# Output weights of seven heads laid out with 32 rows in a partition, and attention output brought into that layout by selecting matmuls

## The chip, the core and the metric

The kernel runs on one core of one Trainium2 chip, in one launch. The metric is the time of an execution on the device, in microseconds. The core has a matmul engine (PE, with its weight loads shown as PEld), a vector engine (DVE), a scalar engine (ACT), GpSimd (POOL), a sync engine that issues DMAs (SP), and 16 DMA engines that serve its queues.

## The reference

One token is decoded. A grouped-query attention over a long cache and a gated feed-forward layer are mixed by one scalar gate. All tensors are bfloat16.

```python
# x (1,1,448); k_cache, v_cache (1,8,65536,256); wq (448,4096); wo (4096,448)
q = (x @ wq).reshape(1, 1, 16, 256).transpose(0, 2, 1, 3)     # 16 query heads
k = jnp.repeat(k_cache, 2, axis=1); v = jnp.repeat(v_cache, 2, axis=1)
p = softmax(einsum("bhqd,bhkd->bhqk", q, k) / 16)
o = einsum("bhqk,bhkd->bhqd", p, v)
a = o.transpose(0, 2, 1, 3).reshape(1, 1, 4096) @ wo
gate = x @ W_gate; up = x @ W_up                              # (448,1792) each
b = (gate * (gate > 0) * up) @ W_down                         # (1792,448)
g = sigmoid((x * gate_w).sum(-1))
out = g * a + (1 - g) * b
```

The two caches hold 537 MB of the 549 MB that are read; `wo` is 3.67 MB.

## The kernel before

The caches are walked head by head (eight cached heads, two query heads each). A head has four K tiles and four V tiles of 16,384 cache rows; a tile is 128 partitions with 64 KB each. Three ring buffers of one tile's size hold them: V tiles use buffer 0 and K tiles alternate between buffers 1 and 2; at the end the last four V tiles use 1 and 2 and `wo` uses buffer 0.

A K tile is transposed on DVE in place, in eight parts (L470), and multiplied by the query on PE (L481, into the PSUM banks `ST`). DVE takes the maximum (L624) and ACT the exponential with the row sums (L626). After a head's fourth K tile comes the head change: the maxima of the partitions are combined (L631 to L640), the probabilities rescaled (L646) and transposed on PE (L651), and the head's sums are combined, by a product with ones (L671) and a reciprocal into `rc` (L672, L674, two columns, one for each query head, with the gate's factor multiplied in). The V tiles are multiplied by the probabilities on PE (L519) into the bank `OP`, in four groups of four partitions.

The output of a head is finished one head later, inside the next head change. DVE copies `OP` to `o_sb` as bfloat16 (L540). Four small products with the selecting columns `emat` (L545, `f_otr`) sum the four partition groups and turn the output so that it stands along partitions, into `T_ps`. DVE multiplies by `rc` and writes four columns of `attnT` (L550, `f_norm`): two columns for each of the two query heads, because partition p holds the output elements 2p and 2p+1. `wo` is loaded in the same way, 256 rows of it to a block with two rows in each of 128 partitions, which is runs of 2 x 896 B:

```python
WO = [(0, 2 * NW), (2 * NW, J - 4), (J - 4, J - 2), (J - 2, J - 1), (J - 1, J)]   # blocks, J = 16, NW = 5
wo_sb[:, lo:hi, :, :], A_wo[lo * 256:hi * 256, :].rearrange("(j p s) n -> p j s n", p=128, s=2)
```

Every product with `wo` (L492, `proj`) multiplies one column of `attnT` by a 224-column half of a `wo` row, accumulating into `A_ps`, two halves in two column groups; the feed-forward result has been put into the same bank early (`f_dn`).

The order of the work is a plan: each operation has an engine, a key (a due time in microseconds from a written-out list `order` with the length of each transfer), and the operations it depends on. Each engine runs its operations in the order of the keys and waits on semaphores. SP issues the transfers in the order of the list: the last full V tiles, the first `wo` transfer (ten blocks), the last V tile in five pieces of 64, 32, 16, 8 and 8 rows of a partition (L688), then four more `wo` transfers (2, 2, 1, 1 blocks). PE multiplies the first `wo` blocks before it meets the pieces of V, and the rest behind the last piece, around the turning of the last head's output. The steps of the heads in the middle stand in loops whose addresses come from a register (`roll`).

Of the kernel before, what the change touches and what calls it, by code (L numbers as in the profile page):

```python
# [25 lines left out]
class _Plan:  # L26
# [8 lines left out]
    def op(self, eng, key, fn, deps=(), tag=None):  # L35
        o = _Op(eng, key, fn, deps, tag=tag)
        self.ops.append(o)
        return o

    def dma(self, eng, key, sem, fn, deps=()):  # L40
        if sem not in self.dsem:
            self.dsem[sem] = self.es.enter_context(self.nc.semaphore("d_" + sem))
        o = _Op(eng, key, fn, deps, dma=sem)
        self.ops.append(o)
        return o
# [167 lines left out]
def bass_gated_mix__gqa_block_cached__glu_gated_reglu__decode_kernel(  # L213
# [35 lines left out]
    with es:  # L249
# [26 lines left out]
        RS = sb("rs", [128, NTH], F32)  # L276
        X = sb("hs", [128, 20], F32)
        rc = sb("rc", [128, 2], F32)
        attnT = sb("attnT", [128, H * 4], BF)
        hT = sb("hT", [128, FT], BF)  # L280


# [27 lines left out]
        VT_ps = M_ps[0:2, 0:128]  # L310
        NMR_ps = M_ps[:, 128:129]
        T_ps = M_ps[:, 480:484]
        GB_ps = M_ps[:, 496:498]
        LS_ps = M_ps[:, 500:502]
        XT_ps = M_ps[:, 504:504 + NX]
# [5 lines left out]
        def mop(*a, **k):  # L321
            o = op(*a, **k)
            touch_m.append(o)
            return o
# [4 lines left out]
        for n in range(3, NT):  # L329
            order.append(("k", n, TILE))  # L330
            if n >= NTH:
                order.append(("v", n - NTH, TILE))
        NW = H - 3
        for i in range(NT - NTH, NT - 1):
            order.append(("v", i, TILE))
        order.append(("wo", 0, 7.3))
        PIECES = [(0, 64), (64, 96), (96, 112), (112, 120), (120, 128)]
        for i, (lo, hi) in enumerate(PIECES):
            order.append(("vp", i, TILE * (hi - lo) / U))

        WO = [(0, 2 * NW), (2 * NW, J - 4), (J - 4, J - 2), (J - 2, J - 1), (J - 1, J)]
        for i in range(1, 5):
            order.append(("wo", i, 0.55 * (WO[i][1] - WO[i][0])))
        t = 3.0
        tL, issue = {}, []
        for kind, i, d in order:
# [15 lines left out]
        for kind, i, _ in order:  # L362
            if kind in ("k", "v") or (kind, i) in (("wo", 0), ("vp", 0)):
                r = place(kind, i)
                slot[kind, i], freed[kind, i] = r, held.get(r, [])
                held[r] = [(kind, i)]
        wo_sb = ring[slot["wo", 0]][:, 0:J * 2 * D].rearrange("p (j s n) -> p j s n", j=J, s=2)


        d_x = dma("ac", -9, "x", lambda e: e.dma_start(x_row, A_x[0, :, :]))  # L370
# [24 lines left out]
            prev = op("gp", 0.3 + 0.01 * w, lambda e, w=w: e.iota(iot1[32 * w:32 * w + 32, :], [[-1, 4]], base=0, channel_multiplier=1), [prev])  # L395
        g_em = op("gp", 0.4, lambda e: e.tensor_scalar(emat[:], iot1[:], 0.0, None, ALU.is_equal), [prev])

        prev = g_em
        for i in range(4):
            prev = op("gp", 0.5 + 0.01 * i, lambda e, i=i: e.tensor_scalar(selc[:, 6 + i:7 + i], iot1[:, 0:1], 4.0 * (i + 1), None, ALU.is_lt), [prev])  # L400
        g1 = op("gp", 0.6, lambda e: e.tensor_tensor(selc[:, 6:7], selc[:, 6:7], selc[:, 8:9], ALU.add), [prev])
# [12 lines left out]
        z6 = mop("pe", 1.6, lambda e: e.matmul(GB_ps, ones_f[0:1, :], gz[0:1, 2:4], start=True, stop=True), [z5, c_one])  # L414
        z7 = mop("dv", 1.7, lambda e: e.tensor_copy(gb[:], GB_ps), [z6])


        def f_xeo(e):
            e.tensor_copy(xeo[0:1, 0:128:2], x_row[0:1, NR3:D])
# [90 lines left out]
        def make_pv(n, lo, hi, sl, tv, dep):  # L510
            h, a = divmod(n, NTH)

            def f_pv(lo, hi):
                return lambda e: f_mm(e, lo, hi)

            def f_mm(e, lo, hi):
                for k in range(lo // 2, hi // 2):
                    g = k % 4
                    ins = e.matmul(OP[32 * g:32 * g + 4, :], pcur[a % 2][:, 4 * k:4 * k + 4],  # L519
                                   ring[sl][:, k * 512:(k + 1) * 512],  # L520
                                   start=False, stop=False, skip_group_check=True,
                                   tile_position=(0, 32 * g))
                return ins
            tp = max(tv, last["tev", h])
            if lo == 0:
                pc[n] = op("ac", tp - 5, lambda e: e.copy(  # L526
                    pcur[a % 2][:].rearrange("p (k i) -> p k i", i=4),
                    ptp[:].rearrange("p (k i f) -> p k i f", i=4, f=4)[:, :, :, a]), last["ev", h] + [pv.get(n - 2)])
            if lo == 0 and a == 0:
                zero_o(last["tev", h] + (0.5 if h else -2), h)  # L530
            deps = [dep, pc[n]] + ([last["zo", h]] if a == 0 and lo == 0 else [])
            if n >= NT - NTH and a == 1:
                for q_, (l2, h2) in enumerate(PIECES):
                    pv[n] = op("pe", tp + 0.1 * q_, f_pv(l2, h2), deps if q_ == 0 else [dep], tag=("tail", 1, q_))
            else:
                tag = ("pv", a % 2, sl) if n < NT - NTH else ("tail", a % 2, 0 if n < NT - 1 else [q_[0] for q_ in PIECES].index(lo))
                pv[n] = op("pe", tp, f_pv(lo, hi), deps, tag=tag)
            if a == NTH - 1 and hi == U:
                tn = tp + (8.0 if n < NT - 1 else 1.2)
                o1 = op("dv", tn, lambda e: e.tensor_copy(o_sb[:], OP[:]), [pv[n], last.get(("otr", h - 1))])  # L540

                def f_otr(e):
                    for s in range(2):
                        for par in range(2):
                            ins = e.matmul(T_ps[:, 2 * s:2 * s + 2], o_sb[:, par * 256 + s:par * 256 + 256:2],  # L545
                                           emat[:, 2 * par:2 * par + 2], start=(par == 0), stop=(par == 1))
                    return ins
                o2 = mop("pe", tn + 0.5, f_otr, [o1, g_em], tag="otr")
                def f_norm(e, at):
                    return e.tensor_tensor(at.rearrange("p (s q) -> p s q", q=2), T_ps.rearrange("p (s q) -> p s q", q=2),  # L550
                                           rc[:, :].unsqueeze(1).to_broadcast([128, 2, 2]), ALU.mult)
                o3 = mop("dv", tn + 1, lambda e: f_norm(e, attnT[:, h * 4:(h + 1) * 4]), [o2, last["rc", h]])
                o3.roll = lambda e, r: f_norm(e, attnT[:, bass.ds(r * 4 - 4, 4)])
                last["ocp", h], last["otr", h], last["norm", h] = o1, o2, o3
                if h < H - 1:
                    last["l4", h + 1].deps.append(o3)
                last["tn", h] = tn + 1

        for kind, i, t in sorted(issue, key=lambda q: q[0] != "wq"):
# [11 lines left out]
            elif kind == "gu":  # L571
# [27 lines left out]
                def f_dn(e):  # L599
                    for ft in range(FT):  # L600
                        ins = proj(e, hT[:, ft:ft + 1], wd_sb[:, ft, :], ft == 0, False)
                    return ins
                l_["dn"] = op("pe", tg + 3, f_dn, [l_["hT"], l_["wd"]])
            elif kind == "wd":
                l_["wd"] = dma("sp", t, "wd", lambda e: e.dma_start(wd_sb, B_W_down.rearrange("(p ft) d -> p ft d", ft=FT)))
            elif kind == "k":
# [22 lines left out]
                if t_ == NTH - 1:  # L629
# [40 lines left out]
                    l2 = op("dv", T + 18.2, lambda e: e.tensor_scalar(X[:, 6:8], selc[:, 0:2], X[:, 5:6], None, ALU.mult), [l1])  # L670
                    l3 = mop("pe", T + 19, lambda e: e.matmul(LS_ps, ones_f[:, :], X[:, 6:8], start=True, stop=True), [l2, c_one], tag="l3")  # L671
                    l4 = mop("dv", T + 19.5, lambda e: e.reciprocal(rc[:, :], LS_ps), [l3])  # L672
                    last["l4", h] = l4
                    l5 = op("dv", T + 19.6, lambda e: e.tensor_scalar(rc[:, :], rc[:, :], gb[:, 0:1], None, ALU.mult), [l4, z7])  # L674
                    last["rc", h] = l5
                    last["tev", h] = T + 20
                    for args in [p_ for p_ in pending if p_[0] // NTH == h]:
# [2 lines left out]
            elif kind in ("v", "vp"):  # L680
                if kind == "v":
                    n, lo, hi = i, 0, U
                    sl = slot["v", n]
                    dep = dma("sp", t, "r%d" % sl, lambda e, sl=sl, n=n: e.dma_start(ring[sl][:], v_src(n)), free(("v", n)))
                else:
                    n, (lo, hi) = NT - 1, PIECES[i]
                    sl = slot["vp", 0]
                    dep = dma("sp", t, ("wq", "wqh", "wd", "wf0", "wf1")[i], lambda e, sl=sl, n=n, lo=lo, hi=hi: e.dma_start(  # L688
                        ring[sl][:, lo * 256:hi * 256], v_src(n)[:, lo * 256:hi * 256]), free(("vp", 0)))
                args = (n, lo, hi, sl, tL[kind, i], dep)  # L690
                if ("tev", n // NTH) in last:
                    make_pv(*args)
                else:
                    pending.append(args)
            elif kind == "wo":
                lo, hi = WO[i]
                l_["wo", i] = dma("sp", t, "wo%d" % i, lambda e, lo=lo, hi=hi: e.dma_start(
                    wo_sb[:, lo:hi, :, :], A_wo[lo * 256:hi * 256, :].rearrange("(j p s) n -> p j s n", p=128, s=2)), free(("wo", 0)))

        LAST = last["tn", H - 1]  # L700
        for i, (lo, hi) in enumerate(WO):
            for h in range(lo // 2, (hi + 1) // 2):
                key = max(tL["wo", i], last["tn", h] + 0.5) + 0.01 * h
                if i == 0:
                    key = tL["vp", 0] - 1 + 0.01 * h
                if i in (1, 2):
                    key = LAST - (0.7, 0.2)[i - 1]
                elif i > 2:
                    key = LAST + 2 + 0.1 * i

                def f_wo(e, h=h, lo=max(lo, 2 * h), hi=min(hi, 2 * h + 2)):
                    for j in range(lo, hi):
                        for s in range(2):
                            c = h * 4 + s * 2 + j - 2 * h
                            ins = proj(e, attnT[:, c:c + 1], wo_sb[:, j, s, :], False, j == J - 1 and s == 1)
                    return ins
                fin = op("pe", key, f_wo, [l_["wo", i], last["norm", h], l_["dn"]])
        f0 = op("dv", T_END, lambda e: e.tensor_copy(fin_o[:, 0:D2], A_ps[0:1, 0:D2]), [fin])
        f1 = op("ac", T_END, lambda e: e.copy(fin_o[:, D2:D], A_ps[32:33, 0:D2]), [fin])
        f2 = dma("sp", T_END + 1, "out", lambda e: e.dma_start(out[0, :, :], fin_o), [f0, f1])  # L720
# [30 lines left out]

        @block.vector
        def _(e):
            pl.emit_heads("dv", progs["dv"], e, [first["dv", h] for h in range(2, H)] + [last["ocp", H - 1]], 2)

        @block.scalar
        def _(e):
# [35 lines left out]
```

## Time and profile before

| | |
|---|---|
| median of 3 runs | 1277.62 us (1277.54 to 1278.2) |
| the profiled execution | 1277.72 us |
| its span, first to last instruction | 1275.9 us |
| mean granted TensorE clock | 0.63 |
| PE, PEld, DVE, ACT busy | 32%, 12%, 50%, 6% of the span |
| DMA | 549.17 MB, mean 430 GB/s, the SP queue 99.7% of 16 engines' span |

A page of the profile gives busy times, the span in 40 slices, the queues, and the chain of work that ended last. Further views give windows (busy time of each engine, granted clock, share of the DMA engines and GB/s in a stretch), the timeline (start, length, engine, line, operation, operands, and in brackets the idle time before it and what ended it), groups of instructions by line (busy time in total and mean ns of one, then the idle time before them), and the DMA issues (count, KB, median us from issue to landing). Times in the timeline and windows count from the start of the span.

### The profile page before, as it was taken

Reading aid. Unit: us, or ns where it says so; the run is one execution under the profiler, and the core shown is the slowest. Engines: PE = TensorE matmul, PEld = TensorE weight load, DVE = VectorE, ACT = ScalarE, POOL = GpSimd, SP = SyncE. Lnnn points to the kernel's source line nnn. Section 1 sums busy time; section 2 is a strip of 40 time slices with the busy share of each in tenths; the row PEclk is TensorE's granted clock in tenths of the full one; section 3 lists DMA queues with packets and bytes.
Section 4 is the critical chain, followed back from the end, with each engine's and each line's share of the span. In section 5 each row is a group of like instructions: output and inputs, shape, how many; then the busy total and the mean of one; then the engine's idle time right before and its main releaser. Section 6 shows DMA issues by size and latency. Waiting matters only on the chain.

```text
span 1275.9 us, 10241 instructions
## 1 busy us (share of the span) xinstructions
PE 403.0 (32%) x4500; PEld 147.3 (12%) x4500; DVE 634.6 (50%) x424; ACT 71.9 (6%) x156; POOL 4.1 (0%) x21
## 2 busy tenths in 40 slices
PE   0343433142332223332223431324321243322515
PEld 0211211010110101111001110101100011100202
DVE  4688555553455633556433755335554355554200
ACT  0000100010000100000000100001000010000100
POOL 1000000000000000000000000000000000000000
PEclk9857665566665566656666655666656666556666
DMA  9999999999999999999999999999999999999998
GB/s 400 453 428 429 430 430 438 436 434 431 431 431 440 434 427 436 429 440 438 427 431 434 436 438 431 431 434 431 440 434 427 436 429 438 438 429 431 434 415 359
DMA packets 12944, 549.17 MB, mean 430 GB/s; under 512 B 1283, under 2 KB 3590, under 8 KB 3974
## 3 DMA queue, kind: packets, MB, share of 16 engines
q1 hardware_dynamic: 12930, 549.03, 99.7%
q8 instruction: 6, 0.10, 0.0%
q14 instruction: 4, 0.03, 0.0%
q10 hardware_dynamic: 4, 0.00, 0.0%
HBM read 549.03 MB, written 0.00 MB: 430 GB/s over the span
## 4 chain that ended last, share of the span: by engine, by line
DVE 37%; another core or an unknown queue 28%; DMA 15%; PE 12%; issue 5%; SPq 1%; ACT 0%; DVEq 0%
DVE ring L470 35%; PE ST L481 8%; DMA ring<-in_A_k_cache_dram 8%; DMA ring<-in_A_v_cache_dram 3%; PE O L519 3%; DMA ring<-in_A_wq_dram 2%; DMA ring<-in_A_wo_dram 2%; SPq L688 1%; DVE P_sb L646 1%; DVE nmb L624 1%; PE M_ps L442 1%; DVE o_sb L540 0%; PE M_ps L671 0%; PE A_ps L492 0%
## 5 line engine op out<-in xcount | busy, mean ns | idle before, releaser
L470 DVE STREAM_TRANSPOSE ring<-ring 128x2048 uint32<-128x2048 uint32 x256 | 565.7, 2275 | 408.5 <-DMA ring<-in_A_k_cache_dram 408.5
L481 PE MATMUL ST<-ring,xcur 128*16 128x512 bf16 x2048 | 223.4, 610 | 760.9 <-DVE ring L470 757.9
L481 PEld LDWEIGHTS ST<-ring,xcur 128*16 128x16 bf16 x2048 | 62.6, 119 | 909.3 <-DVE ring L470 800.1
L519 PE MATMUL O<-ring,pcur 128*4 128x512 bf16 x2048 | 141.6, 436 | 45.9 <-DMA ring<-in_A_v_cache_dram 45.9
L626 ACT ACTIVATE P_sb<-ST,nmb 128x512 bf16<-128x512 f32 x32 | 45.3, 1415 | 1040.6 <-DVE nmb L624 1040.6
L624 DVE TENSOR_REDUCE nmb<-ST 128x1 f32<-128x512 f32 x32 | 22.0, 689 | 106.4 <-PE ST L481 106.4
L519 PEld LDWEIGHTS O<-ring,pcur 128*4 128x4 bf16 x2048 | 54.3, 97 | 137.7 <-issue 90.7
L540 DVE CAST o_sb<-O 128x512 bf16<-128x512 f32 x8 | 5.5, 685 | 72.3 <-PE O L519 72.3
L646 DVE TENSOR_TENSOR P_sb<-P_sb,hs 128x1024 bf16<-128x1024 bf16 x16 | 18.9, 1215 | 6.9 <-ACT hs L640 6.9
L651 PE MATMUL PT<-identb,P_sb 128*128 128x128 bf16 x128 | 12.8, 259 | 21.5 <-DVE P_sb L646 21.5
L526 ACT COPY pcur<-ptp 128x256 bf16<-128x256 bf16 x32 | 14.0, 439 | 32.3 <-PE O L519 32.2
L442 PE MATMUL M_ps<-ring,P_sb 128*128 128x256 bf16 x64 | 8.8, 309 | 18.6 <-DMA ring<-in_A_wq_dram 18.6
L637 DVE TENSOR_REDUCE mx<-M_ps 2x1 f32<-2x128 f32 x8 | 2.2, 279 | 22.4 <-PE M_ps L635 22.4
L651 PEld LDWEIGHTS PT<-identb,P_sb 128*128 128x128 bf16 x128 | 9.3, 116 | 23.7 <-DVE P_sb L646 23.7
L660 ACT COPY ptp<-PT 128x256 bf16<-128x256 bf16 x32 | 10.3, 375 | 25.2 <-PE PT L651 25.2
L442 PEld LDWEIGHTS M_ps<-ring,P_sb 128*128 128x128 bf16 x64 | 7.0, 111 | 20.2 <-issue 18.7
L626 ACT ACTIVATION_READ_ACCUMULATOR P_sb<-ST,nmb 128x1 f32 x32 | 8.5, 265 | 0.0
L550 DVE TENSOR_TENSOR attnT<-M_ps,rc 128x4 f32 (+1 forms) x8 | 1.3, 162 | 7.3 <-PE M_ps L671 6.3
L492 PE MATMUL A_ps<-ring,attnT 128*1 128x224 bf16 x64 | 4.7, 305 | 0.6 <-DMA ring<-in_A_wo_dram 0.6
L506 PE MATMUL O<-zer,identb 128*128 128x512 bf16 x8 | 4.7, 593 | 0.0
L671 PE MATMUL M_ps<-hs,ones_f 128*128 128x2 f32 x16 | 4.4, 344 | 0.0
L671 PEld LDWEIGHTS M_ps<-hs,ones_f 128*128 128x128 f32 x16 | 4.2, 315 | 0.1
(81 smaller groups left out, 58.6 us busy)
## 6 DMA issues: line engine op xcount, KB each, us to landing
ring<-in_A_v_cache_dram SPq DMA_DIRECT2D x1, 4096.0 KB, 29.1
ring<-in_A_wq_dram SPq DMA_DIRECT2D x1, 3072.0 KB, 29.0
ring<-in_A_wo_dram SPq DMA_DIRECT2D x1, 2240.0 KB, 39.0
ring<-in_A_v_cache_dram SPq DMA_DIRECT2D x1, 2048.0 KB, 23.0
ring<-in_B_W_down_dram SPq DMA_DIRECT2D x1, 1568.0 KB, 33.1
ring<-in_B_W_gate_dram SPq DMA_DIRECT2D x1, 1344.0 KB, 30.7
ring<-in_B_W_up_dram SPq DMA_DIRECT2D x1, 1344.0 KB, 33.5
ring<-in_A_v_cache_dram SPq DMA_DIRECT2D x1, 1024.0 KB, 25.0
```

The costliest lines, as they stand in the source:

```text
L442: ins = e.matmul(QN_ps, xw3[:, k_, 31 - j:159 - j], rhs, start=(j == 0 and kt == 0), stop=(j == J - 1 and kt == R3))
L470: return lambda e: e.transpose(v, v)
L481: ins = e.matmul(bank[32 * w:32 * w + 16, :], xcur[:, x0:x0 + 16], ktv[sl][:, u0:u0 + 16, c, :, r_], start=(b == 0 and c == 0 and r_ == 0) ...
L519: ins = e.matmul(OP[32 * g:32 * g + 4, :], pcur[a % 2][:, 4 * k:4 * k + 4], ring[sl][:, k * 512:(k + 1) * 512], start=False, stop=False, s ...
L526: pc[n] = op("ac", tp - 5, lambda e: e.copy(pcur[a % 2][:].rearrange("p (k i) -> p k i", i=4), ptp[:].rearrange("p (k i f) -> p k i f", i= ...
L624: smax[n] = op("dv", sx, lambda e, n=n, t_=t_: e.tensor_reduce(NM[:, t_:t_ + 1], ST[n % 2][:], AX.X, ALU.max, negate=True), [qk[n, 1], las ...
L626: aexp[n] = op("ac", sx + 1, lambda e, n=n, t_=t_: e.activation(P_sb[:, t_:2048:4], ST[n % 2][:], ACTF.Exp, bias=NM[:, t_:t_ + 1], scale=1 ...
L646: rsc = op("dv", tt, lambda e, pb=pb: e.tensor_tensor(pb, pb, X[:, 12:16].unsqueeze(1).to_broadcast([128, 256, 4]), ALU.mult), [h7, aexp[n]])
L651: ins = e.transpose(PT[rd][:, s * 128:(s + 1) * 128], P_sb[:, (rd * 8 + s) * 128:(rd * 8 + s + 1) * 128], identb[:, :])
L660: ins = e.copy(dst, src)
L671: l3 = mop("pe", T + 19, lambda e: e.matmul(LS_ps, ones_f[:, :], X[:, 6:8], start=True, stop=True), [l2, c_one], tag="l3")
L688: dep = dma("sp", t, ("wq", "wqh", "wd", "wf0", "wf1")[i], lambda e, sl=sl, n=n, lo=lo, hi=hi: e.dma_start(ring[sl][:, lo * 256:hi * 256], ...
```

## The change

`wo` of heads 0 to 6 is loaded as 112 partitions with 32 consecutive rows each, in two transfers: rows 0 to 23 of every partition ahead of the last V tile, rows 24 to 31 behind its pieces. The runs are 21,504 and 7,168 B. Head 7's two blocks keep the old layout, in two transfers behind that. The attention output has to stand in the new layout: partition 16h + 8q + d, column s, for element 32d + s of query head q of cached head h. For this, `o_sb` is now divided by the row sum while it is copied from `OP` (the factor stands in `rcr`, one value for each partition, made by the mask `mg` and one more reduction), and 16 selecting products with shifted views of the mask `esel` add a head's two outputs into 32 columns of the bank of `A_ps` (`AX_ps`), which one product with zeros clears before the feed-forward result is accumulated there. One copy takes the columns to `attnA` when head 6 is done. Head 7 is turned as before and copied to `attnZ`. In the loops the shifted view of `esel` is addressed from a register.

```diff
+        g_es = op("gp", 0.405, lambda e: e.memset(esel[:], 0.0), [g_em])
+        for par in range(2):
+            g_es = op("gp", 0.41 + 0.01 * par, lambda e, par=par: e.tensor_copy(
+                esel[:, par, 120:129:8], emat[:, 2 * par:2 * par + 2]), [g_es])
...
+        z8 = op("dv", 1.8, lambda e: e.tensor_tensor(mg[:], emat[:, 0:2], emat[:, 2:4], ALU.add), [g_em])
+        z9 = op("dv", 1.9, lambda e: e.tensor_scalar(mg[:], mg[:], gb[:, 0:1], None, ALU.mult), [z7, z8])
...
-                o1 = op("dv", tn, lambda e: e.tensor_copy(o_sb[:], OP[:]), [pv[n], last.get(("otr", h - 1))])
+                o1 = op("dv", tn, lambda e: e.tensor_scalar(o_sb[:], OP[:], rcr[:, 0:1], None, ALU.mult),
+                        [pv[n], last.get(("otr", h - 1)), last["rc", h]])
+                def f_sel(e, w):
+                    for d_ in range(8):
+                        for par in range(2):
+                            ins = e.matmul(AX_ps, esel[:, par, w(d_)], o_sb[:, par * 256 + d_ * 32:par * 256 + (d_ + 1) * 32],
+                                           start=False, stop=False, skip_group_check=True)
...
-                o3 = mop("dv", tn + 1, lambda e: f_norm(e, attnT[:, h * 4:(h + 1) * 4]), [o2, last["rc", h]])
+                if h < HA:
+                    o2 = op("pe", tn + 0.5, lambda e: f_sel(e, lambda d_: slice(120 - 16 * h - d_, 248 - 16 * h - d_)),
+                            [o1, g_es, l_["axz"]], tag="otr")
+                    o2.roll = lambda e, r: f_sel(e, lambda d_: bass.ds(136 - d_ - r * 16, 128))
+                    last["l5", h + 1].deps.append(o1)
+                else:
+                    o2 = mop("pe", tn + 0.5, f_otr, [o1, g_em])
+                    o2 = mop("dv", tn + 1, lambda e: e.tensor_copy(attnZ[:], T_ps), [o2])
...
+                l_["axz"] = op("pe", tg + 2.9, lambda e: e.matmul(
+                    AX_ps, identb[:, :], zer[:, 0:1].to_broadcast([128, 32]), start=True, stop=True, skip_group_check=True),
...
-                    l5 = op("dv", T + 19.6, lambda e: e.tensor_scalar(rc[:, :], rc[:, :], gb[:, 0:1], None, ALU.mult), [l4, z7])
+                    l5 = op("dv", T + 19.6, lambda e: e.tensor_tensor(rc[:, :], rc[:, :], mg[:, :], ALU.mult), [l4, z9])
+                    l5 = op("dv", T + 19.7, lambda e: e.tensor_reduce(rcr[:, :], rc[:, :], AX.X, ALU.add), [l5])
...
-        WO = [(0, 2 * NW), (2 * NW, J - 4), (J - 4, J - 2), (J - 2, J - 1), (J - 1, J)]
+        HA = H - 1
+        PA = HA * 16
+        SA = 24
+        WO = [(0, SA), (SA, 32), (J - 2, J - 1), (J - 1, J)]
...
+                if i < 2:
+                    fn = lambda e, lo=lo, hi=hi: e.dma_start(
+                        wo_a[:, lo:hi, :], A_wo[0:PA * 32, :].rearrange("(p s) n -> p s n", s=32)[:, lo:hi, :])
+                else:
+                    fn = lambda e, lo=lo, hi=hi: e.dma_start(
+                        wo_z[:, lo - J + 2, :, :], A_wo[lo * 256:hi * 256, :].rearrange("(p s) n -> p s n", s=2))
...
+        aA = op("dv", last["tev", H - 1] + 1, lambda e: e.tensor_copy(attnA[:], AX_ps), [last["otr", HA - 1]])
...
+                if i < 2:
+                    for s_ in range(lo, hi):
+                        ins = proj(e, attnA[0:PA, s_:s_ + 1], wo_a[:, s_, :], False, False)
+                else:
+                    for s_ in range(2):
+                        c = s_ * 2 + lo - J + 2
+                        ins = proj(e, attnZ[:, c:c + 1], wo_z[:, lo - J + 2, s_, :], False, i == 3 and s_ == 1)
...
+            fin = op("pe", LAST + 0.5 + i if i else tL["vp", 0] - 1, f_wo, [l_["wo", i], aA if i < 2 else last["otr", HA], l_["dn"]])
```

## What the change was predicted to do

> **What bounds the kernel now.** I read the page first, its span, slices and queues.
>
> ```profile
> span 1275.9 us, 10241 instructions
> POOL 1000000000000000000000000000000000000000
> DMA  9999999999999999999999999999999999999998
> q1 hardware_dynamic: 12930, 549.03, 99.7%
> ```
>
> The 16 DMA engines are busy for 99.7% of the span and nothing is idle in any slice before the last, so the bytes set the time and only what stands after the last bytes is paid besides. The profiled execution took 1277.72 us, 1.82 more than its span; the median is 1277.62. I sum against 1277.72. Then the chain of waits, its end:
>
> ```profile
> 1244.53 26.59 DMA ring<-in_A_wo_dram
> 1271.16 0.91 PE A_ps L492 x8
> 1272.27 1.68 PE A_ps L492 x16
> 1273.97 0.38 DVE P_sb L718
> ```
>
> The end is a wo transfer landing at 1271.16 and then the last wo products. The rate at which the bytes come is read from the table of windows (busy of PE, PEld, DVE, ACT, POOL, then clock, DMA share, GB/s):
>
> ```profile
> 1200.00:1241.00 41.00, 11.54 (x128) 3.73 (x128) 0.00 (x0) 0.83 (x2) 0.00 (x0) 0.62 1.01 434
> 1244.00:1247.00 3.00, 2.48 (x24) 0.83 (x28) 0.00 (x0) 0.00 (x0) 0.00 (x0) 0.50 1.06 381
> 1250.00:1257.00 7.00, 2.82 (x56) 1.96 (x48) 0.00 (x0) 0.00 (x0) 0.00 (x0) 0.99 1.00 431
> 1270.00:1273.00 3.00, 2.38 (x26) 1.03 (x28) 0.85 (x2) 0.00 (x0) 0.00 (x0) 0.50 0.59 216
> ```
>
> V tiles (64 KB in one run per partition) move at 434 GB/s, which is 27.1 for each of 16 engines; the middle of the first wo transfer (runs of 1,792 B) moves at 381 with the engines just as busy. The sizes, and the end in order of time:
>
> ```profile
> ring<-in_A_wo_dram SPq DMA_DIRECT2D x1, 2240.0 KB, 39.0
> ring<-in_A_wo_dram SPq DMA_DIRECT2D x2, 448.0 KB, 26.7
> ring<-in_A_wo_dram SPq DMA_DIRECT2D x2, 224.0 KB, 21.4
> ```
> ```profile
> 1250.74 2.08 PE L492 MATMUL A_ps<-ring,attnT 128*1 128x224 bf16 x40
> 1269.95 0.59 PE L519 MATMUL O<-ring,pcur 128*4 128x512 bf16 x4 [0.69 <-DMA ring<-in_A_v_cache_dram]
> 1270.61 0.69 DVE L540 CAST o_sb<-O 128x512 bf16<-128x512 f32 x1 [72.31 <-PE O L519]
> 1271.16 0.91 PE L492 MATMUL A_ps<-ring,attnT 128*1 128x224 bf16 x8 [0.61 <-DMA ring<-in_A_wo_dram]
> 1272.01 0.27 PE L545 MATMUL M_ps<-emat,o_sb 128*128 128x2 bf16 x4
> 1272.27 1.66 PE L492 MATMUL A_ps<-ring,attnT 128*1 128x224 bf16 x16
> 1272.31 0.16 DVE L550 TENSOR_TENSOR attnT<-M_ps,rc 128x4 bf16<-128x4 f32 x1 [1.01 <-PE M_ps L545]
> 1273.39 0.09 PEld L492 LDWEIGHTS A_ps<-ring,attnT 128*1 128x1 bf16 x4 [0.29 <-DMA ring<-in_A_wo_dram]
> ```
>
> The last piece of V is met at 1269.95, the first wo transfer behind it at 1271.16, the last at 1273.39; 16 products take 1.66 us (104 ns each), and PE ends at 1273.93, which is 3.79 us before 1277.72.
>
> **Part 1: bytes and runs.** All wo bytes stay: 2240 + 2 x 448 + 2 x 224 KB. Ahead of V's pieces stood 2.294 MB, 6.02 us at 381 GB/s; now 112 x 21,504 B = 2.408 MB, at 434 5.55 us, so 0.47 less. Behind the pieces stood 1.376 MB, 3.61 us; now 112 x 7,168 B = 0.803 MB at 434, 1.85 us, and 0.459 MB still in runs of 1,792 B, 1.20 us: 3.05, 0.56 less. Taken alone the transfers end 1.03 us earlier. SP issues fewer packets (2,048 become 112 + 112 + 256), and the long issues below get shorter:
>
> ```profile
> 1230.82 13.67 SPq L688 DMA_DIRECT2D ring<-in_A_v_cache_dram  x5
> 1244.53 16.67 SPq L697 DMA_DIRECT2D ring<-in_A_wo_dram  x4
> ```
>
> They wait for room in the queue while the engines have work (shares of 1.00 and more above) and end at 1261.2, before the transfers are met. I cost that at nothing.
>
> **Part 2: the products at the end.** The transfer met first behind V's pieces was 448 KB, 1.20 us; it is now 1.85. With 0.47 won ahead, it lands at 1271.16 - 0.47 + 0.65 = 1271.34. Only then may its 16 products start, and 8 more for head 7: 24 x 0.104 = 2.49 us, end at 1273.83 against 1273.93. The cast (now a multiplication by one value per partition, 0.69 us either way: same bank, same elements) and the four products of L545 end by 1271.2, the copy of head 7's output is covered by 16 products, and the wo products of heads 0 to 6, 48 instead of 40 with 0.052 us each (2.5 us from 1250.74 on), are over long before the first V piece is met. So 1.03 us of transfers becomes 0.10 us of time: **1277.6**, if the new transfers run at full rate.
>
> **Part 3: what 112 rows do to the 16 engines.** Every transfer of more than one row in this trace has 128 rows, eight to an engine; no row shows 112. I bound it from both sides. The low end is part 2. The other end: the 434 GB/s may be a limit not of the engines but of the partitions that each of them has to itself, which the 128-row rows can't tell apart. The 1.06 beside 381 speaks a little for it: an engine starts a packet while the one before is unfinished, so it isn't the engine's queue alone that holds it. Seven rows in a row to an engine don't line up with groups of eight, so two engines meet in one group and halve each other. If each engine shares all its rows, the big transfer takes 11.10 us (+5.08 against 6.02) and the small one 3.70 (+2.50 against 1.20): it lands at 1278.74, PE ends at 1281.23, 7.30 late: 1285.0. If half of them, 8.33 (+2.31) and 2.78 (+1.58): 1275.05, 1277.54, 3.61 late: 1281.3. I take the middle, **1283.2**. Towards the other neighbours, a shared row of V's first piece (32 KB at 27.1 GB/s) adds 1.2 us; two of them make the upper bound 1287.4.
>
> [...]
>
> **Part 4: the seven head changes.** Each gets 16 selecting products in place of four, the reciprocal of the next row sum waits behind them on PE (L671 follows them), and one more small reduction on DVE follows. First the groups of instructions (busy, mean ns, idle before), then the timeline:
>
> ```profile
> L545 PE MATMUL M_ps<-emat,o_sb 128*128 128x2 bf16 x32 | 2.1, 170 | 1.5 <-DVE o_sb L540 1.1
> L545 PEld LDWEIGHTS M_ps<-emat,o_sb 128*128 128x128 bf16 x32 | 1.5, 107 | 3.6 <-DVE o_sb L540 3.2 <-issue 0.4
> L669 DVE TENSOR_REDUCE hs<-hs 128x1 f32<-128x4 f32 x8 | 1.3, 157 | 0.3
> ```
> ```profile
> 1191.68 0.08 PEld L635 LDWEIGHTS M_ps<-identf,hs 128*2 128x2 f32 x1 [0.44 <-issue]
> 579.53 0.23 DVE L674 TENSOR_SCALAR rc<-rc,gb 128x2 f32<-128x2 f32 x1
> 585.94 4.50 DVE L470 STREAM_TRANSPOSE ring<-ring 128x2048 uint32<-128x2048 uint32 x2 [6.18 <-DMA ring<-in_A_k_cache_dram]
> ```
>
> A product and its load unpipelined are 0.28 us; twelve more are 3.3 us at most, and by the 0.27 us for four above, 0.8 at least. Each also gets a register instruction for its weights' address, which the trace doesn't show alone: 0.44 us at most, by the gap that held one at a loop's end, 7.0 for 16; by the 0.07 us in which a whole product passes, 1.1. Between 2 and 10 us then, with 0.2 for the reduction, and I take 3. Cover at the smallest of these changes that I read is 6.18 us, in which DVE waits for a K tile. If that is gone, DVE starts up to 4 us late on a tile of 17.7 us in a period of 38.7 (two tiles of 8.39 MB at 434 GB/s), and catches up before the next; nothing queued behind it frees a buffer sooner than SP needs it, since a V transfer is issued 33.0 us ahead of landing for 19.3 us of bytes:
>
> ```profile
> ring<-in_A_v_cache_dram SPq DMA_DIRECT2D x31, 33.0
> ```
> ```profile
> 160.01 17.66 DVE L470 STREAM_TRANSPOSE ring<-ring 128x2048 uint32<-128x2048 uint32 x8 [12.39 <-DMA ring<-in_A_k_cache_dram]
> 110.74 3.28 PE L481 MATMUL ST<-ring,xcur 128*16 128x512 bf16 x32 [8.46 <-DVE ring L470]
> ```
>
> Zero, then. The same for head 0, whose extra reduction is followed by 12.39 us of waiting, and for the one product that clears the selected columns, followed by 8.46. The mask and its copies on GpSimd and two small DVE operations fall into the first slice, where GpSimd's only work lies.
>
> **Rivals.**
> A. *The engines are the limit, not the partitions.* Then part 2 stands alone: 1277.6, not slower. For it: V's first piece, in rows of 32 KB, still moves at 431. With the clock at 0.99 instead of 0.50 in the last products (0.052 instead of 0.104 us for 24, -1.25) it would be 1276.4, still not 0.2% away (2.55 us, about what a measurement can tell from no change).
> B. *112 rows go out as 14 engines with eight rows, or the busiest groups take eight rows at the single rate without meeting.* Big transfer 8 x 21,504 / 27.1 = 6.35 us (+0.33), small one 2.12 (+0.92): 1272.41, PE ends at 1274.90, +0.97: 1278.7. It decides where the work splits evenly by groups. [...]
> C. *The head changes lose their cover.* It decides when the selecting products pass some 20 us, the rest of a K period, far over the 10 of part 4. At 1 us each over it, seven make 7 us: 1284.7. Against it stands all of part 4.
>
> **How the numbers follow.** Engines that meet (the forecast, 1281.3 to 1287.4) 0.62: the one mechanism that the transfers' new shape touches directly. No meeting, A: 0.22. B: 0.09. C, or still fewer engines: 0.03. Something I don't see that wins over 2.55 us: 0.04, since all that the transfers' runs can win is 1.03. Slower by over 0.2% is then 0.62 + 0.03 = 0.65; within 0.2%, A and B, 0.31; faster 0.04. The range begins at A less the spread of some 0.4 of single runs, 1277.2, and ends at 1287.4; the likeliest case alone spans 1281.3 to 1287.4.
>
> **What would show it.** In the windows after the last full V tile, the new transfer should show less than 400 GB/s with all engines busy, and packets of 21,504 B well over 0.8 us. V's last piece should be met 2 to 5 us later than 1269.95, measured back from the end, and the idle time before the last wo products should be laid on wo's DMA. Head changes should show DVE still waiting for K's DMA. I am wrong if the new transfer runs near 430 GB/s: then the end moves by 0.1 us, and the products' 2.5 us is the new last step. I am also wrong if the selecting products end after the K tile has landed and the next transfers on SP come late.

## The result, and the profile after

| | before | changed |
|---|---|---|
| median | 1277.74 us (1277.39 to 1278.2, 6 runs) | 1287.24 us (1286.41 to 1288.11, 6 runs) |
| profiled execution | 1277.72 us | 1286.86 us |
| span | 1275.9 us | 1285.1 us |

The changed kernel takes 1.0075 times as long (95% interval 1.0062 to 1.0088), 9.5 us more. I read first whether anything was lost ahead of the `wo` transfers. The windows from the start to 1241 us, before and then after (columns as in the prediction; the last is GB/s):

```profile
0.00:1241.00 1241.00, 385.13 (x4304) 140.79 (x4304) 633.40 (x421) 71.58 (x155) 4.08 (x21) 0.63 1.00 433
```
```profile
0.00:1241.00 1241.00, 401.13 (x4389) 149.47 (x4389) 633.86 (x425) 71.98 (x155) 4.99 (x24) 0.63 1.00 433
```

PE is busy 16 us more, in the head changes, and the bytes come at the same 433 GB/s: no time is lost there. The end of the chain of waits after, and the windows of the last 40 us:

```profile
1233.03 47.61 DMA ring<-in_A_wo_dram
1280.69 2.42 PE A_ps L507 x24
1283.13 0.38 DVE P_sb L745
```
```profile
1246.00:1250.00 4.00, 3.90 (x40) 1.35 (x44) 0.00 (x0) 0.00 (x0) 0.00 (x0) 0.50 0.98 226
1251.00:1255.00 4.00, 0.63 (x12) 0.09 (x4) 0.00 (x0) 0.00 (x0) 0.00 (x0) 1.00 1.05 253
1257.00:1262.00 5.00, 3.66 (x44) 2.50 (x38) 0.00 (x0) 0.00 (x0) 0.00 (x0) 0.68 0.99 426
1274.00:1278.00 4.00, 1.35 (x12) 0.18 (x8) 0.00 (x0) 0.00 (x0) 0.00 (x0) 0.50 1.00 223
```

The chain still ends with a `wo` transfer and the products behind it. But in the first and the last of these windows, where the 112-row transfers run (in the last one together with V's last packets), the DMA engines are as busy as ever (0.98 and 1.00) and move half as much (226 and 223 GB/s). In between, in the third window, V's first piece comes at 426.

The trace also records each DMA packet, with its size, start and length. The 112 packets of 21,504 B took 1.05 to 1.64 us, 1.48 on average, and at least 16 of them were under way at any time in the first window. With the share of 0.98 that shows no engine idle, and every one of these packets is slow, not a few of them: at the 27.1 GB/s of the prediction one would take 0.79 us. The timeline of the end:

```profile
1230.76 2.24 SPq L715 DMA_DIRECT2D ring<-in_A_v_cache_dram  x5
1277.64 0.60 PE L534 MATMUL O<-ring,pcur 128*4 128x512 bf16 x4 [1.74 <-DMA ring<-in_A_v_cache_dram]
1278.29 0.75 DVE L555 TENSOR_SCALAR o_sb<-O,rcr 128x512 bf16<-128x512 f32 x1 [77.10 <-PE O L534]
1279.10 0.27 PE L568 MATMUL M_ps<-emat,o_sb 128*128 128x2 bf16 x4 [0.86 <-DVE o_sb L555]
1280.69 1.66 PE L507 MATMUL A_ps<-ring,attnA 112*1 112x224 bf16 x16 [1.32 <-DMA ring<-in_A_wo_dram]
1282.13 0.96 PE L507 MATMUL A_ps<-ring,attnZ 128*1 128x224 bf16 x8
```

V's last piece is met at 1277.64 instead of 1269.95, 7.69 us later; the transfer behind it 3.05 us after that instead of 1.21, another 1.84 us. From there to PE's end it is 2.40 us instead of 2.77. PE ends at 1283.09 instead of 1273.93: 9.16 us, against 9.14 us between the two profiled executions. So the whole loss lies in the transfers at the end.

### The profile page after: what moved, and what is told of

It is laid out like the page before. It is cut to its first block, busy times and chain, and to the rows that moved or that the text cites. A ratio compares the mean times of both kernels' runs of the same rounds, so it can differ in the third digit from the quotient of the medians.

```text
span 1285.1 us, 10602 instructions
## 1 busy us (share of the span) xinstructions
PE 421.1 (33%) x4593; PEld 157.4 (12%) x4593; DVE 635.2 (49%) x428; ACT 72.3 (6%) x156; POOL 5.0 (0%) x24
## 4 chain that ended last, share of the span: by engine, by line
DVE 37%; another core or an unknown queue 27%; DMA 17%; PE 13%; issue 5%; ACT 0%; SPq 0%; DVEq 0%
DVE ring L485 34%; PE ST L496 8%; DMA ring<-in_A_k_cache_dram 8%; DMA ring<-in_A_wo_dram 4%; DMA ring<-in_A_v_cache_dram 3%; PE O L534 3%; DMA ring<-in_A_wq_dram 2%; PE A_ps L561 1%; DVE P_sb L672 1%; DVE nmb L650 1%; PE M_ps L457 1%; DVE o_sb L555 0%; PE M_ps L697 0%; PE A_ps L507 0%
## 5 line engine op out<-in xcount | busy, mean ns | idle before, releaser
L555 DVE TENSOR_SCALAR o_sb<-O,rcr 128x512 bf16<-128x512 f32 x8 | 6.0, 746 | 77.1 <-PE O L534 77.1
L561 PE MATMUL A_ps<-o_sb,esel 128*128 128x32 bf16 x112 | 18.6, 206 | 4.8 <-DVE o_sb L555 3.7
L561 PEld LDWEIGHTS A_ps<-o_sb,esel 128*128 x112 | 11.8, 105 | 12.7 <-issue 5.5
L507 PE MATMUL A_ps<-ring,attnA 112*1 112x224 bf16 x64 | 5.8, 368 | 6.2 <-DMA ring<-in_A_wo_dram 6.2
L507 PEld LDWEIGHTS A_ps<-ring,attnA 112*1 112x1 bf16 x64 | 3.8, 117 | 8.1 <-DMA ring<-in_A_wo_dram 6.8
```

The lines of the kernel that those rows point to most:

```text
L507: ins = e.matmul(A_ps[32 * g:32 * g + 1, 0:D2], lhsT, rhs[:, g * D2:(g + 1) * D2], start=start, stop=stop, skip_group_check=True, tile_pos ...
L561: ins = e.matmul(AX_ps, esel[:, par, w(d_)], o_sb[:, par * 256 + d_ * 32:par * 256 + (d_ + 1) * 32], start=False, stop=False, skip_group_c ...
```

## Experiments

The theory, which no trace shows directly: the 112 rows fall on partitions that the DMA engines share. The rivals: the shape of the source (long runs that leave gaps), the work added on PE and DVE, and row counts other than 128 as such. They ran in two groups of four, e1 to e4 and e5 to e8, each beside the kernel before on one chip, which took 1277.78 us (1277.45 to 1278.41) in the first group and 1277.97 us (1277.44 to 1278.57) in the second.

**e1_rows128**: 128 rows in the same runs.

```diff
-        wo_a = ring[slot["wo", 0]][0:PA, 0:32 * D]...
+        wo_a = ring[slot["wo", 0]][:, 0:32 * D]...
-                        wo_a[:, lo:hi, :], A_wo[0:PA * 32, :]...
+                        wo_a[:, lo:hi, :], A_wo[0:128 * 32, :]...
...
```

> The two wo transfers bring 128 rows of 32 instead of 112 (the last 16 rows are those of head 7, loaded twice; the products still use 112 partitions). Runs (21,504 and 7,168 B) and their distance in memory (28,672 B) stay. Shared partitions: with eight rows to an engine the transfer runs at about 430 GB/s, 2.75 MB in 6.3 us, and the time falls to about 1278.7 us. Rival, the source: long runs that leave out 7,168 B of every 28,672 are what is slow, so the rate stays near 235 GB/s and the time is 1287 us or, with a seventh more bytes, up to 1289 us.

Measured 1278.73 us, ratio 1.0008 (0.9998 to 1.0018). A window in the first transfer, and the end of the timeline:

```profile
1244.00:1247.00 3.00, 2.79 (x28) 0.96 (x32) 0.00 (x0) 0.00 (x0) 0.00 (x0) 0.50 1.02 437
```
```profile
1270.06 0.60 PE L534 MATMUL O<-ring,pcur 128*4 128x512 bf16 x4 [0.67 <-DMA ring<-in_A_v_cache_dram]
1272.27 1.66 PE L507 MATMUL A_ps<-ring,attnA 112*1 112x224 bf16 x16 [0.48 <-DMA ring<-in_A_wo_dram]
```

One seventh more bytes, and 8.5 us less than the changed kernel. The 128 packets of 21,504 B took 0.80 to 0.81 us each. (Packets are counted in the window in which they start, so a short window can show a little over 434.) The long runs and the gaps in the source are not the cause: that rival falls.

**e2_old_transfers**: all of the change but the transfers.

```diff
-        WO = [(0, SA), (SA, 32), (J - 2, J - 1), (J - 1, J)]
+        WO = [(0, 20), (20, 24), (24, 28), (J - 2, J - 1), (J - 1, J)]
...
-                        wo_a[:, lo:hi, :], A_wo[0:PA * 32, :].rearrange("(p s) n -> p s n", s=32)[:, lo:hi, :])
+                        wo_a.rearrange("p (j s) n -> p j s n", s=2)[:, lo // 2:hi // 2, :, :],
+                        A_wo[lo * 128:hi * 128, :].rearrange("(j p s) n -> p j s n", p=128, s=2))
...
```

> The changed kernel with the transfers of before (128 rows, runs of 1,792 B, 10 + 2 + 2 + 1 + 1 blocks), which leaves the wo rows in other places than the products take them to be; 40, 8, 8, 4 and 4 products. Everything else of the change stays: selecting products, division first, order of the last products. Shared partitions: 1277.9 us (24 products of 0.104 us behind the turning of head 7 instead of 16, +0.2). Rival, the work: if the selecting products and the longer head changes carry part of the loss, the time stays several us higher, up to 1287 us.

Measured 1277.77 us, ratio 1.0 (0.999 to 1.0009). The end of its chain:

```profile
1271.53 2.35 PE A_ps L507 x24
1273.91 0.38 DVE P_sb L746
```

PE ends as in the kernel before, to 0.05 us. The selecting products, the division first and the new order of the last products cost nothing that shows. The rival of the added work falls.

**e3_short_runs**: 112 rows, but the old runs of 1,792 B.

```diff
-                        wo_a[:, lo:hi, :], A_wo[0:PA * 32, :].rearrange("(p s) n -> p s n", s=32)[:, lo:hi, :])
+                        wo_a.rearrange("p (j s) n -> p j s n", s=2)[:, lo // 2:hi // 2, :, :],
+                        A_wo[0:PA * 32, :].rearrange("(j p s) n -> p j s n", p=PA, s=2)[:, lo // 2:hi // 2, :, :])
```

> The changed kernel with 112 rows, but each partition's 32 wo rows come in 16 runs of 1,792 B as in the kernel before, not in one run (which puts them into other places than the products take them to be). Shared partitions: the rate is as low as with the long runs, some 235 GB/s or below, and the time is 1287 us or more. Rival, the source: runs of 1,792 B moved at 381 GB/s before, so 2.408 MB take 6.3 us and 0.803 MB 2.1 us, and the time is about 1278.7 us.

Measured 1286.98 us, ratio 1.0069 (1.0052 to 1.0086), as slow as the changed kernel:

```profile
1245.00:1251.00 6.00, 4.53 (x44) 1.55 (x48) 0.00 (x0) 0.00 (x0) 0.00 (x0) 0.50 1.07 228
```

Runs that moved at 381 GB/s into 128 partitions move at 228 into 112. What is slow is the way into 112 partitions, in runs of 1,792 B as in those of 21,504 B (226).

**e4_rows120**: 120 rows, 15 times 8 (`PA + 8` for `PA` in the two lines of e1's diff).

> The two wo transfers bring 120 rows (8 more than needed); the products still use 112 partitions. 120 is 15 times 8. Shared partitions, in the prediction's words of groups of eight neighbours: each of 15 engines has a group of eight to itself, the rate is 15/16 of 434, 407 GB/s, and the time about 1278.7 us. [...]

Measured 1290.47 us, ratio 1.0101 (1.0084 to 1.0118).

```profile
1245.00:1251.00 6.00, 4.26 (x56) 1.53 (x60) 0.00 (x0) 0.00 (x0) 0.00 (x0) 0.61 0.98 226
```

Fifteen of its packets of 21,504 B are under way between 1246 and 1250 where the changed kernel has 16, as 15 engines with eight rows each would show, and that doesn't help: 226 GB/s. If the eight rows of an engine are neighbours, groups of eight neighbouring partitions, as the prediction had them, are wrong; which rows an engine takes isn't in the trace. What was left to try was the rival that any count but 128 is slow.

**e5_rows64_low and e6_rows64_mid**: each of the two transfers of 112 rows becomes two transfers of 64, which go into partitions 0 to 63 in e5 and into 32 to 95 in e6. If the count alone is the cause, both are as slow as the changed kernel; if the place is, they can differ.

```diff
...
+                    q4 = ring[slot["wo", 0]][0:64, :]          # e6: [32:96, :]
+                    for half, c0 in ((0, 0), (1, 36 * D)):
+                        fn = lambda e, ...: e.dma_start(
+                            q4[:, c0:c0 + 32 * D].rearrange("p (s n) -> p s n", s=32)[:, lo:hi, :],
+                            A_wo[half * 2048:half * 2048 + 2048, :].rearrange("(p s) n -> p s n", s=32)[:, lo:hi, :])
...
```

> The changed kernel, in which each of the two wo transfers of 112 rows is replaced by two transfers of 64 rows, both into partitions 0 to 63 (other columns), 128 rows in all as in e1_rows128; the products take what lies in partitions 0 to 111 of the first, so they are not those of the reference. [...]

> As e5_rows64_low, but the transfers of 64 rows go into partitions 32 to 95, which the products don't all read. Only the place differs. [...] Rival, the row count: as slow as e5_rows64_low, about 1287 us. [...]

Measured: 1292.54 us (ratio 1.0113, 1.0098 to 1.0129) in partitions 0 to 63, and 1278.84 us (1.001, 1.0 to 1.0019) in 32 to 95. A window of the low one, then of the middle one:

```profile
1245.00:1251.00 6.00, 3.21 (x32) 1.10 (x36) 0.00 (x0) 0.00 (x0) 0.00 (x0) 0.50 1.01 208
```
```profile
1244.00:1247.00 3.00, 2.45 (x24) 0.83 (x28) 0.00 (x0) 0.00 (x0) 0.00 (x0) 0.50 1.02 437
```

Same rows, same bytes, same runs, same count: 208 GB/s in one place and 437 in the other, 13.7 us apart. For 64 rows the count as such is not the cause; the place is. And groups of eight neighbours are out, whichever rows an engine takes: partitions 32 to 95 are eight such groups, which at the 27.1 GB/s that 434 leaves to each of 16 would give 217 GB/s, not 437. That 112 and 120 rows are slow for the same reason is inferred from this; no other place was tried for them. An estimate from the two rates: the 3.67 MB of the four transfers take 17.6 us at 208 GB/s and 8.4 at 437, which is 9.2 of the 13.7 us. In the other 4.5, V's packets around the transfers were slowed too (those of 32 KB took up to 2.98 us, in e6 at most 1.23), as in the changed kernel. How much of that each transfer causes I didn't take apart.

**e7_four_rows**: the kernel before, with longer runs but 128 rows.

```diff
...
+                    wo_4[:, lo // 2:hi // 2, :, :], A_wo[lo * 256:hi * 256, :].rearrange("(h p s) n -> p h s n", p=128, s=4)
...
+                    for s in range(4):
+                        for q in range(2):
+                            for par in range(2):
+                                ins = e.matmul(T_ps[64 * q:64 * q + 64, s:s + 1], o_sb[:, par * 256 + s:par * 256 + 256:4], ...
...
```

> The kernel before, with wo of heads 0 to 6 in runs of 3,584 B (four rows in each of 128 partitions, one block to a head) instead of 1,792 B; head 7 as before. The output is turned by 16 products of 64 columns instead of four, in the head changes, and multiplied in two halves. 128 rows everywhere. Shared partitions: the runs gain what the rate allows; runs of 4,096 B moved at about 412 GB/s and those of 1,792 B at 381, so 2.294 MB take 5.65 us instead of 6.02, and two blocks of 0.459 MB 0.07 us less each: 0.5 us faster, 1277.3 us, no difference that can be told. Rival, the head changes: if 16 products there cost time, it is slower than 1278 us.

Measured 1277.15 us (1277.02 to 1277.43, 11 runs), ratio 0.9995 (0.9986 to 1.0004). A window in the first transfer, and the end:

```profile
1244.00:1247.00 3.00, 2.76 (x28) 0.97 (x32) 0.00 (x0) 0.00 (x0) 0.00 (x0) 0.50 1.08 427
```
```profile
1269.32 0.60 PE L520 MATMUL O<-ring,pcur 128*4 128x512 bf16 x4 [0.69 <-DMA ring<-in_A_v_cache_dram]
1271.53 1.66 PE L493 MATMUL A_ps<-ring,attnT 128*1 128x224 bf16 x16
```

Runs of 3,584 B move at 427 GB/s where those of 1,792 B had 381, and V's last piece is met 0.63 us earlier. Each of its 11 runs is below all 27 of the kernel before, but the interval of the ratio takes in 1: a gain of 0.8 us that isn't settled. That is what longer runs were worth in this try, and it needs no 112 rows.

**e8_split28**: e1 with 28 rows ahead of V's pieces and 4 behind (`SA = 28`).

> e1_rows128 with 28 rows ahead of V's pieces and 4 behind instead of 24 and 8. It tells what of the 0.95 us that e1_rows128 loses against the kernel before lies in the products behind the last piece and what in the 0.46 MB that it loads twice. Products: the transfer behind the pieces is 0.46 MB (1.1 us instead of 2.1), and only 8 + 8 products follow it: 1.4 us later on V's last piece, 1.0 us less behind it and 0.8 us fewer products; 1278 us. Rival, the bytes: the last transfer lands as late as in e1_rows128 and ends it at 1278.7 us.

Measured 1278.77 us, ratio 1.0007 (0.9997 to 1.0016), as e1.

```profile
1271.86 0.60 PE L534 MATMUL O<-ring,pcur 128*4 128x512 bf16 x4 [0.66 <-DMA ring<-in_A_v_cache_dram]
1273.51 0.91 PE L507 MATMUL A_ps<-ring,attnA 112*1 112x224 bf16 x8
1274.21 0.95 PE L507 MATMUL A_ps<-ring,attnZ 128*1 128x224 bf16 x8
```

My expectation missed. The rival's time came, but not for its reason: the products no longer wait for `wo`. They follow the turning of head 7, which follows V's last piece, met 1.80 us later than in e1. The 0.459 MB more that stand ahead of the piece are 1.06 us of that at 434 GB/s; the rest isn't settled, since the two profiled executions differ by 0.49 us where the medians agree. What was saved behind the piece was paid ahead of it.

## Why the prediction was right, and where its sizes were off

**The direction and the place of the loss (part 3)** were right. e1 to e3 show, with everything else held, that the loss lies in the transfers into 112 partitions, and neither in their source nor in the work added. That engines meet on shared partitions is my reading of the slow packets and of e5 and e6, which show that the place among the partitions decides the rate (208 GB/s against 437); for 112 rows it is inferred, and no run shows which partitions an engine writes. **The size was too small**: 5.5 us forecast, 9.5 measured. That the median lies inside the range was close: 0.16 us below the upper end, with two of the six runs above it. Two terms of that sum were mis-sized.

- I took the middle between half and full sharing. The rate, 226 GB/s against 434, is nearly full sharing: 2.408 MB take 10.7 us at it, where full sharing had 11.10 and my middle 9.7. That is 1 us for the big transfer. Why it is nearly all and not half stays open; the packet records name neither the engine nor the partition.
- I let the transfers alone be slow and counted their neighbours only for the upper bound. The window from 1251 to 1255, where V's first piece starts while the big transfer ends, still has 253 GB/s. V's last piece came 7.69 us late, where I had said 2 to 5; the big transfer's rate explains 4.6 of it (10.7 less 6.02). Most of the other 3.1 us is in V's own packets: compared with e1 those of 64, 32 and 4 KB around the two transfers took 0.5, 1.3 and 0.5 us longer for each of 16 engines, 2.3 in all. The upper bound had 2.4 for such neighbours; the forecast had nothing.

**The reason given for the meeting was wrong in one point**: not groups of eight neighbours, by e6. That two engines meet in a group and halve each other was my estimate; no run shows the groups or the meeting. What the runs showed in its place is the length of the packets: 1.48 and 0.48 us on average for the two transfers, at seven to each of 16 engines 13.7 us, where 434 GB/s would take 7.4.

**Parts 1 and 2** hold for transfers that run at full rate. By the same working rival B had 1278.7 us for eight rows at the single rate; e1, which is that case with 128 rows, measured 1278.73, with its transfer met at 1272.27 (1272.41 in the text). The 24 products behind the landing took 2.40 us (2.49). SP's issues got short, 2.24 us instead of 13.67 for the pieces, with 112 packets of `wo` ahead of them instead of 1,280, at no gain, as costed.

**Part 4** holds. The smallest cover, in the changed kernel:

```profile
577.47 0.74 DVE L555 TENSOR_SCALAR o_sb<-O,rcr 128x512 bf16<-128x512 f32 x1
578.55 2.82 PE L561 MATMUL A_ps<-o_sb,esel 128*128 128x32 bf16 x16 [0.82 <-DVE o_sb L555]
581.90 0.17 DVE L698 RECIPROCAL rc<-M_ps 128x2 f32<-128x2 f32 x1 [3.68 <-PE M_ps L697]
585.99 4.50 DVE L485 STREAM_TRANSPOSE ring<-ring 128x2048 uint32<-128x2048 uint32 x2 [3.54 <-DMA ring<-in_A_k_cache_dram]
```

The 16 selecting products take 2.82 us, DVE waits 3.68 us for them and the product with ones behind them, and then still 3.54 us for K's transfer: the cover shrank from 6.18 us, by 2.64 where I took 3, and held. The multiplication that replaced the copy takes 0.74 us, not the 0.69 that I had for it.

**The rivals.** A (no meeting) and C (cover lost) are refuted by the rate and by e2. B falls by the 16 packets under way and by the length of each; its price was right for another kernel.

## What to carry to other kernels

Before longer runs are bought with fewer partitions, look where the rows fall: here a transfer of 112 rows ran at 226 GB/s where one of 128 rows in the same runs had 437, and the runs, twelve times as long as before, didn't make up for it. Keep 128 rows, load a few twice if need be (some 1 us here, at the edge of what these runs can tell from nothing), or lengthen runs inside the 128; and where a kernel is bound by its transfers, price each one at the end by its rate in a window of its own, its neighbours included. Moving bytes from behind the last needed transfer to ahead of it moved the wait in e8, not the end.

## What the runs showed of the hardware that I had not expected

A transfer of 64 rows ran at full rate (437 GB/s in a window of 3 us) in partitions 32 to 95 and at 208 GB/s in 0 to 63. In the slow transfers the share of busy DMA engines stayed near 1 (0.98 at 226 GB/s in the changed kernel, 1.01 at 208 in e5): that number told here that packets were under way, not how fast they moved. And packets of the transfers beside a slow one were slow too: V's packets of 32 KB, 1.22 us each in e1, took up to 2.32 us in the changed kernel.
